# Decayed attention feeding a gated MLP on one core: scores of the first four head pairs in one piece of six banks, and the weight conversions of the start in other places

## The chip, the core and the metric

The kernel runs on 1 core of one Trainium2 chip. The metric is the device time of one execution in microseconds (us), lower is better. Of the kernel before, three runs took 804.63, 805.89 and 807.68 us; the median is 805.89 us. Engines are named as in the profile: PE does matrix products, and transposes as products with an identity matrix, DVE is VectorE, ACT is ScalarE, POOL is GpSimd, and SP issues the transfers (DMA).

## What is computed

The reference has two parts. Attention, for 8 batches of 8 heads with 576 tokens and 64 values each (cut to the core):

```python
scores = scale * np.matmul(q, k.transpose(0, 1, 3, 2))
cum = np.cumsum(np.log(np.clip(f, 0.0001, 1.0)), axis=-1)
scores = np.where(causal, -1e9, scores + cum[..., None] - cum[..., None, :])
attn = np.exp(scores - scores.max(-1, keepdims=True))
attn = attn / (attn.sum(-1, keepdims=True) + 1e-09)
x = np.matmul(attn, v)          # heads side by side: 576 x 512 a batch
```

Then a gated MLP on x of each batch:

```python
h = np.maximum(x @ w_in, 0.0)                  # w_in 512 x 1024
u, v = h[..., :512], h[..., 512:]
v_n = (v - v.mean(-1)) / np.sqrt(v.var(-1) + 1e-06)
v_s = np.einsum('ts,bsd->btd', w_spatial, v_n) + b_spatial[None, :, None]
out = (u * v_s) @ w_out
```

## The kernel before, in words

**Attention.** Two heads of one batch make a pair; there are 32 pairs `P`, four to a batch. `prep(P)` loads the pair's q and k (`qk_t`, 608 KB) and rows of the cumulated decay spread over the partitions (`dk` for each head, `dt` for the last 64 tokens of both), and POOL masks them with `affine_select`. Odd pairs of the first batch have buffers of their own, called `d2`, `t2` and `tl2` (the profile shows them as `d` and `t`); all others share `dk`, `tt` and `tl`.

`scores(P)` takes the queries in blocks of 128, `i` = 0 to 3, with 128(i+1) keys each. PE writes the products into banks `sc`, DVE adds the decay and takes the row minimum in one instruction (`lowest`, line 260), ACT takes the Exp with its row sum (line 298), DVE turns the sums into reciprocals (lines 301 and 302), and `share` (lines 266 and 268) scales the rows. `scores_tail` does the same for the last 64 queries of both heads. `transposes` and `transposes_tail` turn the scaled rows over on PE (`tp`); DVE and ACT copy them by turns into `e` (line 347). `attend` multiplies `e` with v (28 products, line 384), and ACT and DVE split the result into a high part `xh` and a low part `xl` (lines 393 and 394).

In `scores`, the blocks 0, 1 and 2 of both heads make one piece in four banks, and block 3 of both heads makes a second piece, which takes the banks 0 and 1 again once `lowest` has emptied them. `in_one_piece` holds the products of a piece together. `share` is done by ACT for the first two batches and by POOL for the others.

**MLP.** `moe(b)` makes v token tile by token tile (`ps`, five tiles, with the normalisation by DVE, POOL and ACT), then u, then the product with w_spatial (`sph` and `spl`, `spta` and `sptb`), the gate, and the product with w_out. Every operand is a sum of a high and a low part, so a product takes three matmuls.

**Weights.** They come as 64-bit words and are converted on the chip by `load64`: a transfer, an Abs on ACT (line 118), five DVE instructions (lines 119 to 125), an addition on POOL (line 126), a high part by ACT (127) and a low part by POOL (128). `load_first` does four w_in blocks (the half for v) and all of w_spatial during the first batch's attention, and a loop at the end of the kernel deals its steps out between those of `attention(0)`. `load_rest` does the other half of w_in in the v stage of the first batch, and w_out after its u stage.

**What sets the order.** `attention` and `moe` are generators. A loop deals out the steps of batch b's MLP and batch b+1's attention by estimated cost, and a scheduler with a timeline model then orders the instructions of each engine. Each engine and SP work through their own queue in that order, and wait for semaphores at its head. `after(i, mark)` only ties the order, without a wait. The first batch's attention stands in PSUM pools of its own: four banks for `sc` and four for `tp`.

## Time and profile before

One execution was profiled:

| | value |
|---|---|
| time of the profiled execution | 804.53 us |
| its span, first to last instruction | 802.8 us |
| PE busy | 765.6 us, 95% of the span |
| PE weight loads busy | 606.9 us, 76% |
| ACT busy | 438.7 us, 55% |
| DVE busy | 433.3 us, 54% |
| POOL busy | 344.0 us, 43% |
| mean granted PE clock | 0.983 |

The profiled execution was 1.36 us under the median. The span is cut into 40 slices of some 20 us, and for each the page gives the busy tenths of an engine. The chain of waits follows the end of the span back to whatever released each step. An entry such as "L347 ACT COPY e<-tp 128x256 x12 | 4.2, 369" gives line, engine, operation, output and input with shape, count, busy time in us, and the mean of one in ns.

### The profile page before, as it was taken

The numbers are of one execution on the slowest core, as the hardware profiler recorded it, in microseconds if no ns is written. First come the engines' busy times: TensorE is split into PE (matmuls) and PEld (weight loads), VectorE is DVE, ScalarE is ACT, GpSimd is POOL, SyncE is SP. The second block draws the span as 40 slices with busy tenths as digits, with TensorE's granted clock in tenths as the row PEclk, the third lists the DMA queues.
The fourth block names the chain that finished last, engine by engine and source line by source line (L and its number), as shares of the span: only waits on it lengthen the run. The fifth ranks groups of instructions, "written<-read, shape, count | busy, mean of one in ns | idle before, by whom it ended". The sixth has DMA issues, their size and how long they took to land.

```text
span 802.8 us, 14554 instructions
## 1 busy us (share of the span) xinstructions
PE 765.6 (95%) x4934; PEld 606.9 (76%) x4934; DVE 433.3 (54%) x1502; ACT 438.7 (55%) x1172; POOL 344.0 (43%) x641
## 2 busy tenths in 40 slices
PE   7677989899999999999999999999999999999997
PEld 3345668687788777877788878877788867888896
DVE  7846878744744446556564555545554536543322
ACT  3898877765555445545464545544564446542331
POOL 4440573424734335444653337443444436433231
PEclk9789989999999999999999999999999999999999
DMA  8653444223223223233322232332233333201001
GB/s 252 186 176 118 141 135 133 80 92 122 96 96 112 51 96 96 96 123 109 97 93 73 92 109 96 96 107 60 86 89 95 122 118 95 66 24 38 27 1 67
DMA packets 34765, 79.44 MB, mean 99 GB/s; under 512 B 4225, under 2 KB 8321, under 8 KB 34690
## 3 DMA queue, kind: packets, MB, share of 16 engines
q1 hardware_dynamic: 34370, 77.98, 31.5%
q8 instruction: 39, 0.64, 0.3%
q10 hardware_dynamic: 320, 0.52, 0.2%
q14 instruction: 36, 0.29, 0.1%
HBM read 68.73 MB, written 9.75 MB: 98 GB/s over the span
## 4 chain that ended last, share of the span: by engine, by line
PE 73%; DMA 3%; DVE 1%; ACT 1%; issue 1%; POOL 1%; ACTq 0%; POOLq 0%; DVEq 0%; SPq 0%
PE ps L214 42%; PE sc L384 8%; PE sc L285 7%; PE tp L356 7%; PE sc L214 5%; DMA out_dram<-o 3%; PE tp L214 2%; PE tp L368 1%; ACT o L544 1%; DVE tt L260 0%; ACT tt L298 0%; POOL tt L268 0%; DVE w L122 0%; POOL gl L520 0%; DVE wa L121 0%
## 5 line engine op out<-in xcount | busy, mean ns | idle before, releaser
L298 ACT ACTIVATE tt<-tt,nm 128x384 f32<-128x384 f32 (+2 forms) x240 | 133.7, 558 | 85.3 <-DVE nm L260 82.4
L268 POOL TENSOR_SCALAR tt<-tt,sm 128x128 f32<-128x128 f32 x192 | 99.6, 541 | 97.8 <-DVE sm L302 97.1
L520 POOL TENSOR_TENSOR gl<-u,gh 128x256 fp32r<-128x256 f32 (+1 forms) x64 | 51.6, 807 | 145.9 <-ACT gh L519 134.0
L356 PE MATMUL tp<-ident,tt 128*128 128x128 f32 x600 | 105.7, 280 | 7.8 <-DVE e L347 2.7
L384 PE MATMUL sc<-e,vraw 128*64 128x320 f32 (+4 forms) x896 | 97.8, 371 | 7.6 <-ACT e L347 5.9
L356 PEld LDWEIGHTS tp<-ident,tt 128*128 128x128 f32 x600 | 73.5, 141 | 39.8 <-issue 7.4
L384 PEld LDWEIGHTS sc<-e,vraw 128*64 128x64 f32 x896 | 61.4, 141 | 46.9 <-issue 7.0
L347 ACT COPY e<-tp 128x256 f32<-128x256 f32 (+1 forms) x160 | 71.4, 452 | 44.7 <-PE tp L356 41.1
L347 DVE COPY e<-tp 128x384 f32<-128x384 f32 (+1 forms) x160 | 70.7, 445 | 41.7 <-PE tp L356 27.3
L285 PE MATMUL sc<-qk_t 64*128 64x128 f32 (+3 forms) x512 | 89.1, 468 | 3.5 <-DVE nm L260 3.2
L260 DVE CUSTOM_DVE_ANT_1 tt<-sc,dk 128x256 f32<-128x256 f32 (+1 forms) x120 | 66.2, 552 | 47.3 <-PE sc L285 34.2
L214 PE MATMUL ps<-sph,vnh 128*128 128x256 f32 (+1 forms) x240 | 76.3, 318 | 0.8 <-ACT u L494 0.4
L214 PE MATMUL ps<-xh,winh 128*128 128x256 f32 (+1 forms) x232 | 75.7, 326 | 0.0
L214 PE MATMUL ps<-spl,vnh 128*128 128x256 f32 (+1 forms) x240 | 71.5, 298 | 0.0
L214 PE MATMUL ps<-sph,vnl 128*128 128x256 f32 (+1 forms) x240 | 71.2, 297 | 0.0
L214 PE MATMUL ps<-xh,winl 128*128 128x256 f32 (+1 forms) x232 | 70.3, 303 | 0.0
L214 PE MATMUL ps<-xl,winh 128*128 128x256 f32 (+1 forms) x232 | 69.7, 300 | 0.0
L285 PEld LDWEIGHTS sc<-qk_t 64*128 64x128 f32 x512 | 45.1, 190 | 29.9 <-issue 10.5
L214 PE MATMUL ps<-winh,xh 128*128 128x512 f32 x148 | 62.2, 421 | 3.5 <-ACT o L544 2.6
L394 DVE TENSOR_TENSOR xl<-sc,xh 128x256 fp32r<-128x256 f32 x64 | 28.7, 453 | 66.3 <-ACT xh L393 66.3
L214 PE MATMUL ps<-winl,xh 128*128 128x512 f32 x148 | 58.5, 396 | 0.0
L260 DVE CUSTOM_DVE_ANT_0 tt<-sc,dk 128x128 f32<-128x128 f32 (+1 forms) x120 | 49.8, 419 | 13.6 <-PE sc L285 9.7
(179 smaller groups left out, 1721.4 us busy)
## 6 DMA issues: line engine op xcount, KB each, us to landing
qk_t<-in_dram SPq DMA_DIRECT2D x32, 608.0 KB, 5.4
dk<-rows_d SPq DMA_DIRECT2D x60, 320.0 KB, 4.4
vraw<-in_dram SPq DMA_DIRECT2D x32, 320.0 KB, 3.0
dt<-rows_d SPq DMA_DIRECT2D x60, 144.0 KB, 3.5
out_dram<-o SPq DMA_DIRECT2D x32, 256.0 KB, 2.1
w<-in_dram SPq DMA_DIRECT2D x16, 256.0 KB, 3.1
w<-in_dram SPq DMA_DIRECT2D x4, 512.0 KB, 6.4
d<-rows_d SPq DMA_DIRECT2D x4, 320.0 KB, 6.9
```

What stands on the lines that cost most here:

```text
L214: T.matmul(o, l, r, start=st, stop=sp)
L260: return V.tensor_tensor_reduce(out=out, in0=ps, in1=dec, scale=-0.125, scalar=3.0e38, op0=ALU.add, op1=ALU.min, accum_out=acc_)
L268: G.tensor_scalar(out=t, in0=t, scalar1=r, scalar2=1.0, op0=ALU.mult, op1=ALU.mult)
L285: return lambda: T.matmul(ps[:, c:c + n], qk_t[p, n - 128:n], qk_t[p, 640:640 + n], start=True, stop=True)
L298: last["exp", P, h, i] = A.activation(t, t, AF.Exp, bias=nm[h][:, i:i + 1], scale=-1.0, accum_out=sm[h][:, i:i + 1])
L347: copied.setdefault(P, []).append((V.tensor_copy if nev[0] % 2 == 1 else A.copy)(out, ps))
L356: T.transpose(out=tp[:, (i - c) * 128:(i - c + 1) * 128], in_=tt[h][:, TOFF[i] + 128 * c:TOFF[i] + 128 * c + 128], identity=ident)
L368: T.transpose(out=tp[:, j * 128:(j + 1) * 128], in_=tl[:, c * 128:(c + 1) * 128], identity=ident)
L384: return lambda: T.matmul(x[64 * h:64 * h + 64, q0 - s0:q1 - s0], vt[:, c, h, :], e[:, h, e0 + q0:e0 + q1], start=c == 0, stop=c == end)
L394: freed[s0 // 256] = V.tensor_tensor(out=xl[:, s0:s0 + n], in0=ps[:, 0:n], in1=f32(xh[:, s0:s0 + n]), op=ALU.subtract)
L520: G.tensor_tensor(out=gl[j][:, 0:nt], in0=g, in1=f32(gh[j][:, 0:nt]), op=ALU.subtract)
L544: A.copy(o, ps)
```

## The change

It touches the first batch's attention and the weights that are converted beside it.

1. **One piece.** For pairs 0 to 3 all four query blocks of both heads are one piece in six banks: block 3 has the banks 4 and 5. The pool `tp` of that time shrinks from four banks to two. In the code the blocks are taken head by head. In the order that the scheduler makes of it, pair 0 goes partly head by head; in pairs 1 to 3 both heads' 512-wide Exps come first, then both 384-wide ones.
2. **Shares.** For pairs 0 to 3 `share` is done by POOL in place of ACT. Batch 1 keeps ACT.
3. **w_in.** The four blocks of `load_first` are placed at set points of the attention's progress, two of them ahead of the first pair and two after `dk` of pair 0.
4. **Loads.** q and k of pair 1 come after `dk` of pair 0; both `dk` transfers of a pair come ahead of its `dt`; v comes after `dk`.
5. **w_spatial.** It leaves the first batch's attention and is loaded and converted by `load_space` in the five v stages of `moe(0)`, in half rows of 288.

```diff
-    def load_first(ws):
-        for c in range(NJ):
...
+    def load_first(ws, c):
...
+        load64(win_v[:, c, DM:2 * DM, :], winh[:, c, DM:2 * DM], winl[:, c, DM:2 * DM], raw, w[:], t[:],
+               ("dma", 0) if c < 2 else ("dk", 0))
+    def load_space(c):
+        for k0 in (0, 288):
+            raw = mo.tile([128, 288], F32, name="wraw", tag="U", bufs=9)
+            ks = slice(k0, k0 + 288)
+            if c < NB:
+                after(SY.dma_start(out=raw, in_=w_sp[c * 128:(c + 1) * 128, ks]), ("exp", PPB - 1, 1, 0))
+                A.copy(sph[:, c, ks], raw)
+                G.tensor_tensor(out=spl[:, c, ks], in0=raw, in1=f32(sph[:, c, ks]), op=ALU.subtract)
...
         last['dma', P] = SY.dma_start(out=qk_t, in_=qk[P])
+        if P == 1:
+            after(last['dma', P], ('dk', 0))
...
-        SY.dma_start(out=vraw, in_=v[P])
+        after(SY.dma_start(out=vraw, in_=v[P]), ('dk', P))
...
-        if P < 2 * PPB:
+        if PPB <= P < 2 * PPB:
             A.activation(t, t, AF.Copy, scale=r)
...
-        for piece in ((0, 1, 2), (3,)):
+        early = P < PPB
+        for piece in ((0, 1, 2, 3),) if early else ((0, 1, 2), (3,)):
...
-                    at[i, h] = (at[0, h][0], 128) if i == 1 else (bank(i % 3 + h), 0)
+                    n = (4 if early else 0) + h if i == 3 else i + h
+                    at[i, h] = (at[0, h][0], 128, h) if i == 1 else (bank(n), 0, n)
...
+            blocks = [(i, h) for h in range(2) for i in reversed(piece)]
+            for i, h in blocks if early else sorted(blocks, reverse=True, key=lambda x: (x[0], -x[1])):
...
+            if b == 0:
+                load_space(i)
...
-            tc.tile_pool(name="p0t", bufs=4, space=PSUM) as p0t:
+            tc.tile_pool(name="p0t", bufs=2, space=PSUM) as p0t:
...
-            if on and (not won or da <= dw):
+        for c in range(NJ):
+            while da < 0.1 + 0.22 * c:
                 da, on = step(gen, da, t_attn)
-            else:
-                dw, won = step(wgen, dw, 6500.0)
+            load_first(ws, c)
+        while on:
+            da, on = step(gen, da, t_attn)
```

**Where the order moves: PE around the first `attend`.** The rows of before start with pair 0's last transposes for head 1; `t_359` is pair 1's head 0.

```order
L356 MATMUL tp<-ident,tt_83 128x128 x10
L368 MATMUL tp<-ident,tl 128x128 x5
L384 MATMUL sc<-e,vraw 64x320 x2
L384 MATMUL sc<-e,vraw 64x256 x2
L384 MATMUL sc<-e,vraw 64x320 x2
L384 MATMUL sc<-e,vraw 64x128 x2
L384 MATMUL sc<-e,vraw 64x320 x2
L384 MATMUL sc<-e,vraw 64x192 x2
L384 MATMUL sc<-e,vraw 64x64 x2
L356 MATMUL tp<-ident,t_359 128x128 x10
L285 MATMUL sc<-qk_t 128x384 x2
```

In the changed kernel the same place reads as follows; `t_327` is pair 1's head 0.

```order
L375 MATMUL tp<-ident,tl 128x128 x5
L363 MATMUL tp<-ident,t_327 128x128 x3
L391 MATMUL sc<-e,vraw 64x320 x2
L391 MATMUL sc<-e,vraw 64x256 x2
L391 MATMUL sc<-e,vraw 64x320 x2
L391 MATMUL sc<-e,vraw 64x128 x2
L391 MATMUL sc<-e,vraw 64x320 x2
L391 MATMUL sc<-e,vraw 64x192 x2
L391 MATMUL sc<-e,vraw 64x64 x2
L363 MATMUL tp<-ident,t_327 128x128 x7
L292 MATMUL sc<-qk_t 128x512 x2
L292 MATMUL sc<-qk_t 128x384 x2
```

Three transposes of the next pair have moved ahead of `attend`, and the scores of the pair after next begin with the 512-wide products. The same holds for the second and third `attend`.

**POOL between the shares of pair 0 and of pair 1.** Before, POOL had no shares here; `w_345` and `w_412` are w_in blocks, `d_642` and `d_643` pair 3's decay rows.

```order
L128 TENSOR_TENSOR winl<-w_345,winh 128x512
L233 AFFINE_SELECT dk<-dk 128x2x128
L235 AFFINE_SELECT dk<-dk 128x256
L126 TENSOR_TENSOR w_412<-w_412,wa 128x512
L233 AFFINE_SELECT dk<-dk 128x2x128
L235 AFFINE_SELECT dk<-dk 128x256
L233 AFFINE_SELECT d_642<-d_642 128x2x128
L235 AFFINE_SELECT d_642<-d_642 128x256
L128 TENSOR_TENSOR winl<-w_412,winh 128x512
L233 AFFINE_SELECT d_643<-d_643 128x2x128
```

In the changed kernel, `w_586` and `w_760` are the third and fourth w_in block, `d_607` pair 3's decay rows of head 0, `t_327` pair 1's rows to be scaled.

```order
L240 AFFINE_SELECT dk<-dk 128x256
L244 AFFINE_SELECT dt<-dt 64x64
L126 TENSOR_TENSOR w_586<-w_586,wa 128x512
L244 AFFINE_SELECT dt<-dt 64x64
L128 TENSOR_TENSOR winl<-w_586,winh 128x512
L238 AFFINE_SELECT d_607<-d_607 128x2x128
L240 AFFINE_SELECT d_607<-d_607 128x256
L126 TENSOR_TENSOR w_760<-w_760,wa 128x512
L273 TENSOR_SCALAR t_327<-t_327,sm 128x128
L273 TENSOR_SCALAR t_327<-t_327,sm 128x256
L273 TENSOR_SCALAR t_327<-t_327,sm 128x384
L273 TENSOR_SCALAR t_327<-t_327,sm 128x512
```

The shares of pair 1 now stand on POOL behind two w_in blocks and behind pair 3's decay rows.

**ACT where the first batch's attention ends.** Before, the last `xh` of the batch follows the shares of pair 4 (`tt_83`) and three instructions of w_in blocks.

```order
L266 ACTIVATE tl<-tl,sm 128x576
L127 CAST winh<-w_985 128x2x128
L266 ACTIVATE tt_83<-tt_83,sm 128x128
L266 ACTIVATE tt_83<-tt_83,sm 128x256
L266 ACTIVATE tt_83<-tt_83,sm 128x384
L266 ACTIVATE tt_83<-tt_83,sm 128x512
L127 CAST winh<-w_998 128x2x128
L118 ACTIVATE wa<-w_1099 128x256
L393 CAST xh<-sc 128x256
L393 CAST xh<-sc 128x320
```

In the changed kernel:

```order
L271 ACTIVATE tt_82<-tt_82,sm 128x512
L354 COPY e<-tp 128x2x2x64
L271 ACTIVATE tt_83<-tt_83,sm 128x128
L271 ACTIVATE tt_83<-tt_83,sm 128x256
L271 ACTIVATE tt_83<-tt_83,sm 128x384
L271 ACTIVATE tt_83<-tt_83,sm 128x512
L118 ACTIVATE wa<-w_949 128x256
L145 CAST sph<-wraw 128x288 x5
L118 ACTIVATE wa<-w_962 128x256
L145 CAST sph<-wraw 128x288 x2
L400 CAST xh<-sc 128x256
```

The last copy into pair 3's `e` stands behind the shares of pair 4's head 0, and the batch's last `xh` behind seven casts of w_spatial.

More of the change, by code (lines that the diff above doesn't have):

```diff
@@ new lines, in load_first @@
+    def load_first(ws, c):
+        raw = ws.tile([128, DM, 2], U32, name="w64")
+        w = ws.tile([128, DM], U32, name="w32")
+        t = ws.tile([128, DM], U32, name="wa")
+        load64(win_v[:, c, DM:2 * DM, :], winh[:, c, DM:2 * DM], winl[:, c, DM:2 * DM], raw, w[:], t[:],
[8 more added lines that the diff above has]
+                G.tensor_tensor(out=spl[:, c, ks], in0=raw, in1=f32(sph[:, c, ks]), op=ALU.subtract)
+            else:
+                for p0 in (0, 64):
+                    after(SY.dma_start(out=raw[p0:p0 + 64, :], in_=w_sp[TL:S, ks]), ("exp", PPB - 1, 1, 0))
+                A.copy(spta[:, ks], raw)
+                V.tensor_tensor(out=sptb[0:64, ks], in0=raw[0:64, :], in1=f32(spta[0:64, ks]), op=ALU.subtract)
+                br = mo.tile([1, 288], F32, name="br", tag="U", bufs=9)
+                bs = [mo.tile([1, 288], F32R, name=f"bs{r}", tag="U", bufs=9) for r in range(2)]
+                after(SY.dma_start(out=br, in_=b_sp[:, ks]), ("exp", PPB - 1, 1, 0))
+                A.copy(bs[0][:], br)
+                V.tensor_tensor(out=bs[1][:], in0=br, in1=f32(bs[0][:]), op=ALU.subtract)
+                for r in range(2):
+                    SY.dma_start(out=f32(sptb[64 + r:65 + r, ks]), in_=f32(bs[r][:]))
@@ L228, in prep @@
         for h in range(2):
-            SY.dma_start(out=dk[h][:, 0:640], in_=row_of(P, h, 0, 640, 128))
+            last['dk', P] = SY.dma_start(out=dk[h][:, 0:640], in_=row_of(P, h, 0, 640, 128))
+        for h in range(2):
             SY.dma_start(out=dt[64 * h:64 * h + 64, :], in_=row_of(P, h, 640, S, 64))
@@ L291, in scores @@
             yield 250 + 1.68 * 128 * sum(i + 1 for i in piece)
[L292 to L299 removed]
+            blocks = [(i, h) for h in range(2) for i in reversed(piece)]
+            for i, h in blocks if early else sorted(blocks, reverse=True, key=lambda x: (x[0], -x[1])):
+                ps, c, m = at[i, h]
+                n = 128 * (i + 1)
+                t = tt[h][:, TOFF[i]:TOFF[i] + n]
+                freed[m] = lowest(t, ps[:, c:c + n], decay(dk[h], i), nm[h][:, i:i + 1])
+                last["exp", P, h, i] = A.activation(t, t, AF.Exp, bias=nm[h][:, i:i + 1], scale=-1.0,
+                                                    accum_out=sm[h][:, i:i + 1])
         for h in range(2):
@@ L398, in attn_gmlp_kernel, with attention @@
     xs = {}
-    def attention(b, ws=None):
+    def attention(b):
         for P in range(b * PPB, (b + 1) * PPB):
```

41 lines of the change are left out of this document (2 added, 39 removed).

## The prediction

> **What bounds the kernel now.** I read the page's clock line and the stretches first, to find where PE isn't the limit; then the timeline of PE over the first batch; then the groups of ACT, DVE and POOL for prices. Columns of the stretches: PE, PEld, DVE, ACT and POOL busy, then PE clock, DMA share, GB/s.
>
> ```profile
> PEclk9789989999999999999999999999999999999999
> 0.00:20.00 20.00, 15.07 (x67) 6.82 (x68) 14.60 (x24) 7.66 (x11) 9.61 (x20) 1.00 0.82 252
> 20.00:40.00 20.00, 12.93 (x53) 6.81 (x52) 16.13 (x62) 16.94 (x50) 9.94 (x19) 0.74 0.63 186
> 40.00:60.00 20.00, 15.52 (x100) 9.71 (x101) 9.81 (x39) 19.58 (x51) 8.27 (x13) 0.83 0.57 179
> 60.00:80.00 20.00, 15.95 (x120) 11.28 (x116) 12.52 (x54) 17.17 (x50) 1.24 (x4) 1.00 0.37 118
> ```
>
> The clock is below 9 tenths only in the first eight of forty slices, so all that this change can gain or lose lies there: later PE simply works through its list. From 40 to 60 us ACT is the limit (19.58 of 20 us), and POOL is nearly free from 60 on (1.24).
>
> ```profile
> 41.25 4.61 PE L384 MATMUL sc<-e,vraw 128*64 128x320 f32 x28 [2.71 <-ACT e L347]
> 45.79 1.31 PE L356 MATMUL tp<-ident,t 128*128 128x128 f32 x10
> 47.03 1.57 PE L285 MATMUL sc<-qk_t 64*128 64x384 f32 x12
> 48.53 1.31 PE L356 MATMUL tp<-ident,t 128*128 128x128 f32 x10
> 49.68 1.14 PE L214 MATMUL sc<-qk_t 128*128 128x288 f32 x4
> 50.74 1.13 PE L285 MATMUL sc<-qk_t 64*128 64x512 f32 x4
> 51.80 0.77 PE L368 MATMUL tp<-ident,tl 128*128 128x128 f32 x5
> 55.80 4.42 PE L384 MATMUL sc<-e,vraw 128*64 128x320 f32 x28 [3.23 <-ACT e L347]
> 69.13 2.93 PE L384 MATMUL sc<-e,vraw 128*64 128x320 f32 x28 [1.63 <-ACT tl L324]
> 81.46 0.50 PE L214 MATMUL ps<-winh,xh 128*128 128x512 f32 x1
> 85.76 2.93 PE L384 MATMUL sc<-e,vraw 128*64 128x320 f32 x28
> ```
>
> The four `attend` start at 41.25, 55.80, 69.13 and 85.76: a pair takes 14.55, 13.33 and 16.63 us, the last with about 4.2 us of the v stage in it (18 products from 81.46). Two of them wait for copies by ACT, and after 2.71 and 3.23 us of idle the same 28 products take 4.61 and 4.42 us, cold, against 2.93.
>
> **The change part by part.** Start. The decay rows of pair 0 pass through DRAM, and its first `lowest` waits for them:
>
> ```profile
> 12.96 0.33 SPq L229 DMA_DIRECT2D dk<-rows_d x1
> 19.12 0.54 DVE L260 CUSTOM_DVE_ANT_0 tt<-sc,dk 128x384 f32<-128x384 f32 x1
> DMA to landing us min/median/max: 4.1/5.0/6.2
> ```
>
> Four transfers leave the queue ahead of them or move behind `dk` (pair 1's q and k, a piece of w_spatial, v, the third w_in block): over 1 MB, at the 252 GB/s of the first stretch up to 4.8 us. The lower end is no gain. `dk` of pair 0 took 6.2 us from issue to first use, the median landing is 5.0; I take 3 us: first `lowest` at 16.
>
> Shares on POOL. ACT loses eight blocks a pair and POOL gains them:
>
> ```profile
> 57.04 3.71 ACT L266 ACTIVATE tt<-tt,sm 128x128 f32<-128x128 f32 x8
> L268 POOL TENSOR_SCALAR tt<-tt,sm 128x128 f32<-128x128 f32 x192 | 99.6, 541 | 97.8 <-DVE sm L302 97.1
> L235 POOL TENSOR_SCALAR_AFFINE_SELECT dk<-dk 128x256 f32<-128x256 f32 x60 | 25.4, 423 | 0.0
> L126 POOL TENSOR_TENSOR w<-w,wa 128x512 f32<-128x512 f32 x4 | 5.5, 1362 | 9.3 <-DVE wa L125 9.3
> L128 POOL TENSOR_TENSOR winl<-w,winh 128x512 fp32r<-128x512 f32 x4 | 5.3, 1315 | 0.1
> ```
>
> By the order, the first `attend` now stands behind three transposes of pair 1, and these behind pair 1's shares. From POOL's first `dk` mask (about 1 us ahead of the first `lowest`, at 15) to those shares, its queue holds 14 masks of 423 ns (5.9 us), six small ones (an estimate of 1.4, from half that size), three additions of 1362 (4.1), three low parts of 1315 (3.9) and pair 0's eight shares with a tail (8 x 541 ns, and an estimate of 0.7 for the tail from the 541 of its smaller kin: 5.0): 20.3 us, so 35.3. Pair 3's decay rows among them can be fetched only when pair 1's `lowest` has let go of the buffer; I add 0.8 us of waiting (bounds 0 and the 5.0 of a landing). Three shares of 541 and the transposes make 1.9 more: the first `attend` at 38 instead of 41.25, **-3.25**.
>
> One rule of the Trainium skill speaks against putting work on POOL here. First its row: the same instruction on the same tile, free, and beside POOL's subtraction of w_spatial.
>
> ```profile
> 10.63 0.69 DVE L125 SCALAR_TENSOR_TENSOR wa<-w,wa 128x512 f32<-128x512 uint32 x1
> 13.36 1.77 DVE L125 SCALAR_TENSOR_TENSOR wa<-w,wa 128x512 f32<-128x512 uint32 x1
> ```
>
> It costs 1.08 us more. The sum takes nothing for it, since `lowest` reads PSUM; bound: eight such instructions of the third and fourth block, 8.6 us of DVE. "SBUF — State Buffer", section "Who interferes with whom", says that DVE and GpSimd share one pair of ports as an exclusive lock, so that a DVE instruction with two SBUF inputs, or in a two-port mode, waits out GpSimd's. The trace agrees in these two rows; by that rule the conversions between the pairs stretch by up to that bound.
>
> The cycle of a pair. Since the transposes stand ahead of `attend`, one chain runs through: `attend`, scores of the pair after next, `lowest`, Exps, shares, transposes, next `attend`.
>
> ```profile
> L260 DVE CUSTOM_DVE_ANT_1 tt<-sc,dk 128x512 f32<-128x512 f32 x4 | 2.7, 680 | 0.0
> L298 ACT ACTIVATE tt<-tt,nm 128x512 f32<-128x512 f32 x4 | 2.9, 714 | 0.9 <-DVE nm L260 0.9
> L298 ACT ACTIVATE tt<-tt,nm 128x384 f32<-128x384 f32 x4 | 2.4, 612 | 1.0 <-DVE nm L260 1.0
> L298 ACT ACTIVATE tt<-tt,nm 128x256 f32<-128x256 f32 x4 | 2.0, 501 | 0.1
> L298 ACT ACTIVATE tt<-tt,nm 128x128 f32<-128x128 f32 x4 | 1.6, 398 | 0.0
> L324 ACT ACTIVATE tl<-tl,nm 128x576 f32<-128x576 f32 x4 | 3.1, 769 | 0.0
> L347 ACT COPY e<-tp 128x512 f32<-128x512 f32 x8 | 4.6, 579 | 1.1 <-PE tp L356 1.1
> L347 ACT COPY e<-tp 128x256 f32<-128x256 f32 x12 | 4.2, 369 | 0.0
> ```
>
> `attend` 2.93; then 1.24 to the scores as now (45.79 to 47.03) and 0.5 for two `tp` banks instead of four; 1.13 and a handover for the two 512-wide products (1.3); `lowest` 0.7; on ACT eight Exps (2 x 0.714 + 2 x 0.612 + 2 x 0.501 + 2 x 0.398 = 4.45), the tail's 0.77, a wide copy of 0.58 and two narrow of 0.37 (6.5 in all); transposes 0.5. That is 13.7 us; the shares (1.5 after the first head's last Exp) fit beside the tail. The first cycle starts cold (+1.6). In the third, the batch's last copy into `e` stands behind eight Exps and a tail (5.2), copies (1.3), the tail's share (0.8) and half of 3.71 (1.9); with 2.93, 1.74, 1.05 and 0.7 ahead of them, 15.6. Sum 15.3 + 13.7 + 15.6 = 44.6, against 85.76 - 41.25 = 44.5 now: **+0.1**. The scores' single piece and the relief of ACT are eaten by the chain's new order.
>
> v stage. The 18 products are no longer ahead of the fourth `attend`: **+4.2**. And PE has waited some 4 us for that copy, so it starts cold: **+1.6** (bounds 0 and 1.7).
>
> Later pairs, in batch 1:
>
> ```profile
> 107.18 0.55 PE L368 MATMUL tp<-ident,tl 128*128 128x128 f32 x3 [0.76 <-DVE e L347]
> 110.31 0.88 PE L356 MATMUL tp<-ident,tt 128*128 128x128 f32 x2 [2.57 <-ACT tt L266]
> 110.00:115.00 5.00, 4.70 (x17) 3.90 (x19) 3.91 (x12) 4.98 (x12) 3.51 (x6) 0.51 0.80 243
> 115.00:120.00 5.00, 5.00 (x40) 3.40 (x39) 1.68 (x6) 3.63 (x10) 3.38 (x8) 0.81 0.32 88
> ```
>
> Here PE stands 0.76 + 2.57 us for pair 5's copies and shares, and then runs cold: 0.49 of 4.70 us and 0.19 of 5.00 us. Together 6.6 us. In the new order four tiles of u stand ahead of those transposes instead of one, which covers the wait: **-6.0** (bounds 0, if u waits for its own w_in blocks instead, and -6.6).
>
> w_spatial. Eight casts and subtractions by ACT and POOL, and four DVE instructions, enter the v stage. The casts ahead of the last `xh` fall into the cold `attend`: **+0.3** (bounds 0, and the late loads of the third rival). What they cost at their old place is in ACT's 19.58 us, which no longer decides.
>
> Sum: -3.25 + 0.1 + 4.2 + 1.6 - 6.0 + 0.3 = -3.05. The profiled execution took 804.53 us (span 802.8), 1.36 under the median of 805.89. So 801.5 against its own time, and with half of the scatter back **802.3** against the median, 0.4% less. About 0.5%, 4.0 us, is what a measurement of this kernel can tell from no change.
>
> **The rivals.**
>
> *The chain is loose and PE sets the pace.* If POOL runs ahead, the transposes ahead of `attend` never wait. PE's work for a pair is 2.93 + 1.31 + 1.57 + 1.31 + 1.14 + 1.13 + 0.77 = 10.2 us; at 11, 11 and 13.5 a cycle, 9 us go: 793. For it: ACT has 4.5 us less a pair. Against: eight Exps and the tail must end before the next transposes.
>
> *POOL's ports and the stall of batch 1.* DVE's conversions stretch beside POOL's shares, pair 1's `lowest` comes up to 4 us later, and the first `attend` again near 41: 806. For it: 1.77 against 0.69. Against: DVE has slack between pairs (9.81 of 20 us). The rule quoted above gives this case.
>
> *Late loads of w_spatial (slower).* By SP's order these pieces are issued only after pair 5's first `dk`, which waits for pair 4's last `lowest`, about 4.5 us ahead of the fourth `attend`. Seven casts stand ahead of `xh` on ACT.
>
> ```profile
> wraw<-in_dram SPq DMA_DIRECT2D x4, 288.0 KB, 7.2
> ```
>
> With nine transfers at 0.5 us of issue, and 7.2 us to land, the seventh comes 2.6 us after the end of that `attend`; the last row with the bias, two round trips of about 3 us, then holds the next Relu on the same queue: 8.7 us, 811. It decides if the seventh piece lands over 4.6 us after the start of the fourth `attend`. Against: these pieces have half the size.
>
> That the change doesn't do what it says: the Exps of pairs 1 to 3 are not taken head by head. That is in the sum already.
>
> **How the numbers follow.** Forecast 802.3, chance 0.46, own range 798 to 806; just under half of it lies over 0.5% faster. Loose chain, 793: 0.20. Ports or stall, 806: 0.16, mostly within 0.5%. Late loads, 811: 0.18. Faster by over 0.5%: 0.22 + 0.20 = 0.42; within: 0.24 + 0.12 = 0.36; slower: 0.04 + 0.18 = 0.22. The range of 8 in 10 reaches from 790, past the loose chain, to 811.
>
> **What would show it.** Right: first `attend` near 38, pairs of 13 to 16 us with PE waiting on POOL's shares or ACT's copies ahead of `attend`, no idle of over 2 us near 105 to 112. Wrong: first `attend` before 34, or cycles below 12 (loose chain); DVE's conversions over 1.5 us each at 22 to 36 (ports); ACT waiting over 2 us for `wraw` (late loads). If the copy of the batch's last `e` doesn't wait behind pair 4's shares, the terms +4.2 and +1.6 are wrong.

## The result and the profile after

The changed kernel takes 815.03 us (median of 4 runs, 814.92 to 815.67) against 805.26 us for the kernel before on the same chip: a ratio of 1.0118, 95% interval 1.0094 to 1.0142. That is slower by 1.2%, outside the predicted range. The profiled execution has a span of 813.2 us against 802.8, so 10.4 us are to be found.

The clock line and the stretches of the kernel after, to be held against those of before (columns as there):

```profile
PEclk9689899999999999999999999999999999999999
0.00:20.00 20.00, 17.00 (x67) 7.32 (x68) 12.73 (x32) 8.71 (x17) 7.05 (x21) 1.00 0.74 226
20.00:40.00 20.00, 11.54 (x45) 6.49 (x45) 14.99 (x52) 11.94 (x37) 18.57 (x30) 0.69 0.68 220
40.00:60.00 20.00, 16.57 (x101) 9.98 (x102) 8.65 (x37) 8.69 (x28) 11.72 (x23) 0.80 0.41 107
60.00:80.00 20.00, 16.25 (x116) 10.48 (x113) 13.23 (x59) 12.13 (x38) 6.63 (x16) 1.00 0.21 68
100.00:120.00 20.00, 15.28 (x71) 11.10 (x69) 18.30 (x46) 12.65 (x33) 13.01 (x19) 0.91 0.17 54
```

ACT is relieved as foreseen (8.69 of 20 us at 40 to 60, where it was 19.58). But POOL is now full at 20 to 40 (18.57), and DVE nearly so at 100 to 120 (18.30). Of the kernel before, the prediction read no stretch between 80 and 110 us. Here is the one of 20 us that matters, and its first half:

```profile
100.00:120.00 20.00, 16.67 (x92) 12.08 (x91) 15.47 (x45) 15.64 (x38) 14.76 (x23) 0.83 0.46 133
100.00:110.00 10.00, 6.97 (x37) 4.78 (x35) 9.88 (x28) 7.03 (x18) 7.86 (x11) 1.00 0.36 101
```

Before the change already DVE worked 9.88 of 10 us just ahead of the stall near 110. The prediction did not read that row, and it bears on much of what follows.

PE in the kernel after, from just ahead of the first `attend` to the first product of the v stage:

```profile
38.30 0.47 PE L363 MATMUL tp<-ident,tt 128*128 128x128 f32 x1 [0.91 <-DVE sm L332]
38.56 1.49 PE L375 MATMUL tp<-ident,tl 128*128 128x128 f32 x5
40.57 0.87 PE L363 MATMUL tp<-ident,t 128*128 128x128 f32 x3 [0.52 <-ACT e L354]
41.38 4.52 PE L391 MATMUL sc<-e,vraw 128*64 128x320 f32 x28
...
56.76 3.67 PE L391 MATMUL sc<-e,vraw 128*64 128x320 f32 x28
...
70.89 2.92 PE L391 MATMUL sc<-e,vraw 128*64 128x320 f32 x28
...
82.55 1.30 PE L375 MATMUL tp<-ident,tl 128*128 128x128 f32 x5 [2.11 <-DVE sm L308]
85.81 4.49 PE L391 MATMUL sc<-e,vraw 128*64 128x320 f32 x28 [1.95 <-ACT e L354]
90.23 0.50 PE L216 MATMUL ps<-winh,xh 128*128 128x512 f32 x1
```

The fourth `attend` starts at 85.81, where it started at 85.76 before; it is cold (4.49 against 2.93), and the first v product comes after it. So up to here nothing is gained, and with 18 products (4.2 us) still to do, the kernel is behind. Cut at the first and the fourth `attend`, the span falls into three pieces: start 41.38 (41.25 before), three cycles 44.43 (44.51), and 727.4 behind the fourth `attend` (717.0). All 10.4 us lie in the last: 4.2 for the products, 1.6 for the cold `attend`, and 4.6 more, where the prediction had 5.7 less.

### The profile page after: what moved, and what is told of

Same layout as the page of the kernel before. It is cut to its first block, busy times and chain, and to the rows that moved or that the text cites. A ratio compares the mean times of both kernels' runs of the same rounds, so it can differ in the third digit from the quotient of the medians.

```text
span 813.2 us, 14613 instructions
## 1 busy us (share of the span) xinstructions
PE 771.2 (95%) x4927; PEld 608.4 (75%) x4928; DVE 434.0 (53%) x1504; ACT 421.0 (52%) x1142; POOL 366.3 (45%) x681
## 4 chain that ended last, share of the span: by engine, by line
PE 69%; issue 5%; ACT 3%; DMA 2%; POOL 2%; DVE 2%; POOLq 0%; ACTq 0%; DVEq 0%
PE ps L216 39%; PE sc L391 8%; PE tp L363 7%; PE sc L292 7%; PE sc L216 5%; PE tp L216 2%; DMA out_dram<-o 1%; ACT tt L305 1%; POOL gl L529 1%; PE tp L375 1%; DVE tt L265 1%; POOL tt L273 1%; DMA dt<-rows_d 1%; ACT gh L528 1%; ACT tt L271 0%
## 5 line engine op out<-in xcount | busy, mean ns | idle before, releaser
L305 ACT ACTIVATE tt<-tt,nm 128x384 f32<-128x384 f32 (+3 forms) x240 | 133.6, 558 | 107.0 <-DVE nm L265 105.4
L273 POOL TENSOR_SCALAR tt<-tt,sm 128x128 f32<-128x128 f32 x208 | 109.0, 541 | 118.0 <-DVE sm L309 109.6
L363 PE MATMUL tp<-ident,tt 128*128 128x128 f32 x600 | 113.9, 285 | 19.0 <-ACT e L354 5.7
L265 DVE CUSTOM_DVE_ANT_1 tt<-sc,dk 128x512 f32<-128x512 f32 (+1 forms) x120 | 66.0, 551 | 60.2 <-PE sc L292 44.5
```

Source lines behind the costliest of these rows:

```text
L265: return V.tensor_tensor_reduce(out=out, in0=ps, in1=dec, scale=-0.125, scalar=3.0e38, op0=ALU.add, op1=ALU.min, accum_out=acc_)
L273: G.tensor_scalar(out=t, in0=t, scalar1=r, scalar2=1.0, op0=ALU.mult, op1=ALU.mult)
L305: last["exp", P, h, i] = A.activation(t, t, AF.Exp, bias=nm[h][:, i:i + 1], scale=-1.0, accum_out=sm[h][:, i:i + 1])
L363: T.transpose(out=tp[:, (i - c) * 128:(i - c + 1) * 128], in_=tt[h][:, TOFF[i] + 128 * c:TOFF[i] + 128 * c + 128], identity=ident)
```

## The experiments

The table has all runs, cut in the same way. "Start" is the start of the first `attend`, "cycles" from there to the fourth, "behind" from the fourth to the end of the profiled span; the ratio is to the kernel before, with its 95% interval. In kernels built on that of before, 4.2 us of v products lie in "cycles"; in those built on that of after, "behind".

Two cautions go with it. The three pieces come from one profiled execution of each kernel, which lies up to 2.3 us off the median of its runs (e4: 810.35 against 812.68), so small differences of pieces are rough. And the scheduler lays the whole order anew for each edit: ahead of the first `attend`, PE does no transpose of pair 1 in the kernel before, three in that after, four in e11 and e14, and nine in e5 and e19. A run shows what an edit does together with the order that comes with it.

| run | median us | ratio | start | cycles | behind |
|---|---|---|---|---|---|
| before | 805.26 | | 41.25 | 44.51 | 717.0 |
| after | 815.03 | 1.0118 (1.0094 to 1.0142) | 41.38 | 44.43 | 727.4 |
| e1 after, w_spatial in pairs 2 and 3 | 813.42 | 1.0109 (1.0087 to 1.0131) | 41.99 | 48.67 | 720.3 |
| e6 after, the same behind pair 2's Exps | 812.33 | 1.0085 (1.0065 to 1.0104) | 41.47 | 47.35 | 721.7 |
| e10 e6, low parts on DVE | 813.32 | 1.0101 (1.0084 to 1.0118) | 41.52 | 51.09 | 718.8 |
| e18 after, w_spatial not converted | 814.39 | 1.0112 (1.0086 to 1.0137) | 44.46 | 44.87 | 723.3 |
| e5 before, w_spatial in the v stage | 814.12 | 1.0118 (1.0100 to 1.0136) | 44.70 | 41.69 | 725.3 |
| e19 before, w_spatial not converted | 806.24 | 1.0019 (1.0002 to 1.0036) | 46.29 | 41.80 | 716.3 |
| e2 after, shares on ACT | 816.85 | 1.0153 (1.0134 to 1.0173) | 42.51 | 42.98 | 728.7 |
| e4 after, pair 4's shares on POOL | 812.68 | 1.0097 (1.0074 to 1.0119) | 41.25 | 42.39 | 724.9 |
| e11 after, pair 0's shares on ACT | 807.58 | 1.0041 (1.0025 to 1.0057) | 42.45 | 39.17 | 722.3 |
| e17 e4 and e11 together | 813.29 | 1.0111 (1.0091 to 1.0131) | 41.35 | 39.39 | 732.4 |
| e14 after, POOL's masks behind the shares | 808.19 | 1.0051 (1.0034 to 1.0069) | 41.24 | 39.88 | 723.7 |
| e3 after, two pieces and four `tp` banks | 810.34 | 1.0063 (1.0044 to 1.0081) | 42.51 | 41.37 | 724.7 |
| e12 e3, e4 and e10 together | 807.46 | 1.0038 (1.0017 to 1.0058) | 42.37 | 42.56 | 720.4 |
| e9 e4, w_spatial behind the 2nd v tile | 812.85 | 1.0091 (1.0070 to 1.0112) | 41.94 | 44.83 | 724.2 |
| e8 e9, all of w_in in the pairs | 812.97 | 1.0106 (1.0081 to 1.0131) | 44.66 | 50.71 | 715.7 |
| e13 before, batch 1's shares on POOL | 808.87 | 1.0041 (1.0024 to 1.0058) | 41.86 | 44.66 | 719.6 |
| e15 after, lighter conversions | 807.12 | 1.0035 (1.0020 to 1.0050) | 41.53 | 44.20 | 717.6 |
| e16 before, lighter conversions | 801.14 | 0.9957 (0.9942 to 0.9973) | 41.23 | 44.75 | 712.1 |

### Where w_spatial is converted

**e1** puts w_spatial back beside the pairs, in whole rows.

```diff
-            if b == 0:
-                load_space(i)
...
-            load_first(ws, c)
+            (load_first, space_first)[k](ws, c)
```

> The changed kernel, with w_spatial converted during the second and third pair (whole rows of 576, as the kernel before did it) and no longer in the v stage. Theory A, w_spatial: its ten loads and twelve casts hold ACT's queue behind transfers at 90 to 103 us, w_in's second half is converted late, and DVE piles up. Then the waits for xh (1.07 us at 94) and for the lowest of pair 5 (2.43 us at 111.6) go, and the kernel takes 807 to 809 us. Theory B, the order: PE comes to the v stage late and cold (85.81 us, 18 products still ahead) whatever is converted there; then 812 to 815. The first four attends stay within 1 us of 41.4, 56.8, 70.9, 85.8 under both.

Behind the fourth `attend` 7.1 us go, and 4.2 come back in the cycles: the time falls little. **e6** moves its loads later, behind the last Exp of the third pair.

```diff
+            after(SY.dma_start(out=raw, in_=w_sp[c * 128:(c + 1) * 128, :]), ("exp", 2, 1, 0))
```

> The changed kernel, with w_spatial converted in whole rows during the third and fourth pair, its loads behind pair 2's last Exp. In the first such run, with it one pair earlier, the second cycle grew from 15.4 to 19.6 us and the fourth attend came at 90.66 in place of 85.81, but what follows it was 7.0 us shorter. Theory A, w_spatial belongs where POOL and ACT have slack (POOL is busy for 6.6 of 20 us from 60 to 80): cycles grow by 1 to 2 us only, the fourth attend comes at 86 to 88, the rest stays 7 us shorter, 807 to 809 us. Theory B, four more subtractions on POOL ahead of its shares cost a pair what they save later, wherever they stand: fourth attend near 90, 812 to 814.

The same picture with smaller numbers: 2.9 more in the cycles, 5.7 less behind. **e10** asks if the subtraction on POOL, between the shares, makes the cycles long.

```diff
-            G.tensor_tensor(out=spl[:, c, :], in0=raw, in1=f32(sph[:, c, :]), op=ALU.subtract)
+            V.tensor_tensor(out=spl[:, c, :], in0=raw, in1=f32(sph[:, c, :]), op=ALU.subtract)
```

> As the run with w_spatial in the third and fourth pair (812.3 us, fourth attend at 88.82), but its four 128x576 subtractions stand on DVE in place of POOL. Theory G, POOL is what made w_spatial dear there (1.46 us each on POOL ahead of masks and shares; 0.75 us on DVE, which has slack): the fourth attend comes at 85.5 to 87, the rest stays, 808.5 to 811 us. Rival, the casts on ACT or the transfers delay the pairs: fourth attend at 88 to 89.5, 811.5 to 814.

It doesn't: on DVE the cycles get 3.7 us longer still. **e5** makes this one move alone, in the kernel before.

```diff
-        for c in range(NB):
-            raw = ws.tile([128, S], F32, name="wraw", bufs=3)
...
+            if b == 0:
+                load_space(i)
```

> The kernel before with only one part of the change: w_spatial converted in the first batch's v stage. Theory A: the same pile-up there, so 809 to 813 us against 805.3, with ACT waiting for wraw between 80 and 105 us. Theory B: what w_spatial leaves free on ACT and POOL in the first pairs is worth as much as it costs later, 804 to 806.

There the move alone costs about as much as the whole change: 8.3 us behind the fourth `attend`, 3.5 at the start, less 2.8 in the cycles. The last two can't be read singly, as nine transposes of pair 1 now stand ahead of the first `attend`; the fourth starts 0.6 us later than before (86.39 against 85.76). Behind it PE waits for `xh`:

```profile
42.33 2.44 PE L359 MATMUL tp<-ident,t 128*128 128x128 f32 x9 [1.08 <-ACT t L269]
...
95.08 0.80 PE L217 MATMUL ps<-winh,xh 128*128 128x512 f32 x1 [2.17 <-ACT xh L396]
```

On ACT `xh` stands there behind three casts, 1.2 us in all. The casts in turn stand behind pair 4's shares, which begin only at 89.41, after ACT has waited 2.44 us for the sums on DVE. So the casts are the smaller part of this wait.

**e9** moves the pieces behind the second v tile (and takes e4's edit, below); **e8** also brings the second half of w_in into the first four pairs.

```diff
-                after(SY.dma_start(out=raw, in_=w_sp[c * 128:(c + 1) * 128, ks]), ("exp", PPB - 1, 1, 0))
+                after(SY.dma_start(out=raw, in_=w_sp[c * 128:(c + 1) * 128, ks]), ("vn", 1))
```

> The changed kernel with pair 4's shares on POOL (as in the run that took 812.7) and w_spatial converted behind the v stage, its loads behind the second tile of v. Theory A, what costs is that twelve casts wait for transfers in ACT's queue ahead of xh and of w_in's second half: the fourth attend at 83.6, then no wait for xh over 0.5 us, 805 to 808 us. Theory D, the work itself is too much for DVE between 95 and 125 us (19.7 of 20 us busy from 100 to 120 in that run), wherever it stands there: 810 to 813.

> As the run before, and w_in's second half is converted during the first four pairs in blocks of 128x512 too, where DVE is busy for 8.7 and 13.2 of 20 us (40 to 60, 60 to 80); w_out follows behind the fourth tile of v. Theory D, DVE's pile from 95 to 125 us is what PE waits for: four blocks of 2.6 us leave it there, the waits of PE between 90 and 165 us fall below 4 us together, and the kernel takes 798 to 803 us if the cycles of the pairs grow by 1 us each. If the conversions stand ahead of lowest and copies in the pairs' chain, cycles grow by 3 us and more, and it takes 805 to 810.

e9 gives nothing over e4 alone. e8 has the second half of w_in out of the v stage (w_spatial is still converted there) and takes 11.7 us less behind the fourth `attend` than after, 8.5 less than e9; it pays 9.6 us for it in start and cycles. By the medians, 812.97 and 812.85, these conversions cost as much in the pairs as in the v stage.

**e18** and **e19** leave the conversion of w_spatial out, in the kernel after and before; the spatial products then multiply zeros.

```diff
+    for d in (sph, spl, spta, sptb):
+        G.memset(f32(d[:]), 0.0)
...
-            if b == 0:
-                load_space(i)
```

> The changed kernel without any conversion of w_spatial: its tiles are filled with zeros by POOL at the very start, so the spatial products multiply zeros; their number and size stay. It gives the whole price of w_spatial in the v stage. Theory E: that price is the 5.6 us by which the stretch behind the fourth attend got longer. Then the four attends stay within 0.5 us of 41.4, 56.8, 70.9 and 85.8, the wait for the last product's xh (1.07) and the ACT waits for wraw are gone, and the median is 809.4. Rival: the stretch is long because the second half of w_in is loaded 9 us later, behind pair 5's rows, whatever ACT does: 814 to 815. Third: both together, and w_in's conversions also come free from POOL's and ACT's queues, 806.

> The kernel before without any conversion of w_spatial, filled with zeros at the start in the same way. It gives the price of w_spatial at its old place, which the prediction took as nothing once the shares had left ACT. Theory: ACT was the limit at 40 to 60 us (19.58 of 20), and five casts of about 0.7 us, three of them there, cost 2 to 3 us between the first and the fourth attend: 802.5 to 803.5. Rival: they lay beside other waits, and the time is that of before within 1 us. Together with the run on the changed kernel: moving w_spatial costs the difference of the two prices, and 5.6 less 2 to 3 would be a net loss of about 3 us.

The fills that I put on POOL at the start spoil both totals. DVE and POOL in e18, then the same DVE instruction in the kernel after:

```profile
3.67 3.39 DVE L79 TENSOR_SCALAR ft<-ft 64x576 f32<-64x576 f32 x1 [2.22 <-DMA ft<-in_dram]
```
```profile
...
3.69 2.02 POOL L104 MEMSET spl<- 128x2304 f32 x1
...
6.17 0.57 POOL L104 MEMSET sptb<- 66x576 f32 x1
```
```profile
3.53 0.45 DVE L79 TENSOR_SCALAR ft<-ft 64x576 f32<-64x576 f32 x1 [2.09 <-DMA ft<-in_dram]
```

The decay, ahead of everything, takes 3.39 us instead of 0.45 beside them, and the first `attend` comes 3.1 us later. In e19 it comes 5.0 later, with nine transposes of pair 1 ahead of it besides the fills. The fourth `attend` in e18, then in e19:

```profile
89.33 4.56 PE L393 MATMUL sc<-e,vraw 128*64 128x320 f32 x28 [1.96 <-ACT e L356]
```
```profile
88.09 2.92 PE L367 MATMUL sc<-e,vraw 128*64 128x320 f32 x28
```

At its new place w_spatial costs 727.4 - 723.3 = 4.1 us behind the fourth `attend`, less than theory E's 5.6. The rival hit the total of e18, but by the fills: 3.1 of its 812.6 us. At its old place it cost 717.0 - 716.3 = 0.7 us behind; what it cost in the cycles is not shown. They are 44.51 - 41.80 = 2.7 us shorter without it, which looks like the theory's 2 to 3, but they begin behind the nine transposes. To the fourth `attend` the fills cost 3.5 us in e18, and in e19 it comes 2.3 us later than before, so by this estimate about 1 us is left for the old place. Without w_spatial in either kernel the rest of the change costs 812.6 - 804.4 = 8.2 us: 1.2 up to the fourth `attend` (89.33 against 88.09) and 7.0 behind it (723.3 against 716.3), of which 5.8 are the products and the cold `attend`. By this pair of runs the move of w_spatial costs the other 2.2 us; e5, in the kernel before and with another order, has 8.9. The runs don't settle which of the two holds.

### The shares, and what holds the first attend

**e2** gives the shares of the first four pairs back to ACT, and **e4** gives those of pair 4 to POOL too.

```diff
-        if PPB <= P < 2 * PPB:
+        if P < 2 * PPB:
```
```diff
-        if PPB <= P < 2 * PPB:
+        if PPB < P < 2 * PPB:
```

> The changed kernel, with the shares of the first four pairs back on ACT. Theory C, POOL's queue delays the start: in the changed kernel pair 0's shares stand behind w_in's low parts and masks on POOL (PE waits 5.42 us for them at 25.0) and pair 1's from 39.49; on ACT they would start some 3 us earlier, and the first attend comes at 38 to 39. But ACT then has 4.5 us more in each cycle: cycles of 16 to 18 us in place of 15.4, 14.1 and 14.9, so 816 to 822 us in all. If POOL's shares do not set the pace of the cycles either, cycles stay below 15.5 and the time is 811 to 813.

> The changed kernel, with the shares of pair 4 (the first of the second batch) on POOL too. The last copy into e of pair 3 then no longer stands behind a tail's and four blocks' shares on ACT (83.0 to 85.4 us): the fourth attend starts at 82.5 to 83.5 in place of 85.81 and runs warm (2.93 in place of 4.49). If that reaches the end: 811 us. Theory A says the v stage's conversions set the pace after it, so that PE waits for them instead: 813.5 to 815, with longer waits for xh near 90.

In e2 the cycles shrink by 1.5, but start and "behind" grow by 1.1 and 1.3, and neither forecast is met. In e4 ACT's copy no longer stands behind pair 4's shares, the fourth `attend` comes 2.2 us earlier and is warm (2.93); the median falls by about 2 us.

**e11** gives only pair 0's shares to ACT (theory C: POOL's queue holds the first `attend`).

```diff
-        if PPB <= P < 2 * PPB:
+        if P == 0 or PPB <= P < 2 * PPB:
```

> The changed kernel, with only pair 0's shares on ACT, which is idle from 21.9 to 25.5 us there. Theory C, POOL's queue sets the first attend (pair 1's shares begin at 39.49 us behind 25.5 us of masks, additions, low parts, pair 0's shares and waits): 5.8 us leave that queue, and the first attend comes at 37.5 to 39.5 in place of 41.4; it then takes 811 to 813 us. Rival, the cold PE, the copies into e and ACT's own queue between 25 and 41 set it: first attend at 41 or later, 814 to 817.

POOL is relieved, and yet the first `attend` is later. POOL:

```profile
37.16 0.41 POOL L238 TENSOR_SCALAR_AFFINE_SELECT d<-d 128x256 f32<-128x256 f32 x1 [4.71 <-DVE sm L332]
```
POOL stands idle for 4.71 us, so its work isn't what holds it here. Pair 1's shares still begin at 39.13, hardly earlier than after's 39.49: in POOL's order they stand behind pair 3's masks, and pair 3's rows are fetched late. So theory C, that POOL's work holds the start, fails. What shrinks is the cycles, to 39.17, and "behind", by 5.1 us; the total of 807.58 lies below both forecasts. The order of the engines changed with the edit, as in e14.

**e14** sets pair 3's masks and the last w_in addition behind pair 1's shares on POOL (theory I).

```diff
-            G.affine_select(out=two, in_=two, compare_op=ALU.is_ge, fill=-8.0 * BIG, base=0,
-                            pattern=[[0, 2], [-1, 128]], channel_multiplier=1)
+            after(G.affine_select(out=two, in_=two, compare_op=ALU.is_ge, fill=-8.0 * BIG, base=0,
+                            pattern=[[0, 2], [-1, 128]], channel_multiplier=1), ('share', P - 2 if P == 3 else -1))
...
```

> The changed kernel, with pair 3's masks on POOL, and the last addition of w_in's first half, put behind pair 1's shares. With pair 0's shares off POOL the first attend did not come earlier (42.45), though POOL then stood idle for 4.7 us: pair 3's rows are fetched only when pair 1's lowest has released the buffer (32.9), their masks start at 37.0 and stand ahead of pair 1's shares. Theory I, that wait sets the start: shares begin at 37.8 (the reciprocals end there) in place of 39.49, the first attend comes at 39.3 to 40.3, 811 to 814 us. Rival, PE's cold transposes and the copies set it: 41 or later, and 814 to 817.

POOL and PE of e14:

```profile
38.23 4.10 POOL L273 TENSOR_SCALAR t<-t,sm 128x128 f32<-128x128 f32 x8 [0.87 <-DVE sm L309]
```
```profile
38.70 0.47 PE L363 MATMUL tp<-ident,tt 128*128 128x128 f32 x1 [0.69 <-DVE sm L332]
38.96 1.50 PE L375 MATMUL tp<-ident,tl 128*128 128x128 f32 x5
40.25 1.06 PE L363 MATMUL tp<-ident,t 128*128 128x128 f32 x4
41.24 4.39 PE L391 MATMUL sc<-e,vraw 128*64 128x320 f32 x28
```

Pair 1's shares start 1.3 us earlier than after's 39.49, and `attend` gains 0.14: pair 0's own transposes and its tail fill PE's queue up to 40.25. The first `attend` has two bounds close to each other, POOL's queue and the transposes of pair 0 with their copies; taking one away shows the other. That the second comes from the two `tp` banks is not shown: e3 has four banks, and its first `attend` starts at 42.51.

What e14 shows beyond its question is larger. It has all the work of the kernel after, on the same engines, and only POOL's order is tied. Yet it takes 808.19 us against 815.03, below both forecasts: the fourth `attend` starts at 81.12, 4.7 us earlier, and 3.7 less follow behind it. ACT in the kernel after, then in e14, the last copy into pair 3's `e` and the first cast of `xh`:

```profile
85.40 0.36 ACT L354 COPY e<-tp 128x256 f32<-128x256 f32 x1
...
93.91 0.36 ACT L400 CAST xh<-sc 128x256 fp32r<-128x256 f32 x1
```
```profile
80.04 0.36 ACT L354 COPY e<-tp 128x256 f32<-128x256 f32 x1
...
86.94 0.37 ACT L400 CAST xh<-sc 128x256 fp32r<-128x256 f32 x1
```

In the kernel after, the copy stands behind the first of pair 4's shares, and `xh` behind seven casts of w_spatial. In e14 the copy comes ahead of those shares, and `xh` behind two casts. So a good part of the loss, some 5.4 us by the ratios, goes with the order that the scheduler laid, by these rows on ACT above all, and not with the work that was moved.

**e17** joins e4 and e11.

```diff
-        if PPB <= P < 2 * PPB:
+        if P == 0 or PPB < P < 2 * PPB:
```

> The changed kernel, with pair 0's shares on ACT (807.6 us alone) and pair 4's on POOL (812.7 alone, against 815.0). If both gains add up: 803.5 to 805.5, the fourth attend at 79 to 80 us. Theory H, what is saved in the pairs is eaten behind them: 806 to 809.

The fourth `attend` starts at 80.74, 5.1 us earlier than after, and all of that goes again behind it. PE:

```profile
106.61 0.69 PE L363 MATMUL tp<-ident,tt 128*128 128x128 f32 x2 [4.09 <-ACT e L354]
...
119.54 4.34 PE L391 MATMUL sc<-e,vraw 128*64 128x320 f32 x28 [2.71 <-DVE e L354]
```

### The pieces and the banks

**e3** takes the scores of the first four pairs in two pieces again, with four `tp` banks; **e12** adds e4's shares and e10's w_spatial.

```diff
-        early = P < PPB
+        early = False
...
-            tc.tile_pool(name="p0t", bufs=2, space=PSUM) as p0t:
+            tc.tile_pool(name="p0t", bufs=4, space=PSUM) as p0t:
```

> The changed kernel, with the scores of the first four pairs in two pieces of four banks again, and four banks for the transposes. Theory E, the two banks cost more than the single piece saves: PE's waits for copies into e between 30 and 41 us (0.90, 0.64, 0.41, 0.52 us) go, the first attend comes at 39 to 40, cycles stay, 811 to 813 us. If the single piece carries the cycles: cycles of 16 us and more, 816 to 820. If neither: within 1 us of 815.0.

> What the runs so far favour, together: scores in two pieces with four transpose banks (cycles 3.1 us shorter in sum), pair 4's shares on POOL (4 us), w_spatial in the third and fourth pair with its subtractions on DVE (5.6 us off what follows the fourth attend, 1 to 3 on the cycles). If they add up: fourth attend at 82.5 to 84.5, warm, and 801 to 805 us, about the kernel before. Theory H, work moved out of one stage only fills another (DVE, ACT and POOL together bound the first 165 us): 806 to 810.

e3 shortens the cycles by 3.1 us and lengthens the start by 1.1, so the fourth `attend` comes 1.9 us earlier than after. Pieces and banks were changed together, so it doesn't say which of them does it. e12 is the fastest of the complete kernels built on that of after, beside e11, and still above before.

### DVE behind the fourth attend

**e13** takes the shares of batch 1 from ACT in the kernel before. If ACT's shares and copies made the stall near 110, it goes.

```diff
-        if P < 2 * PPB:
+        if P < PPB:
```

> The kernel before, with the shares of pairs 4 to 7 on POOL in place of ACT. It measures the stall on which the prediction put 6 us: there PE waits 2.57 us at 110.3 for pair 5's shares on ACT, then runs cold. If that wait was ACT's, it goes and with it the cold stretch: 798 to 801 us against 804.7. Theory D, DVE was late there anyway (9.88 of 10 us busy from 100 to 110): 803 to 806.

It stays, at 1.45 us instead of 2.57 and with DVE as the releaser, and DVE is fuller. The kernel gets slower (808.87), which neither forecast had. Shares on POOL also run beside DVE's conversions, some of which take 1.2 to 1.4 us there, so the run doesn't part ACT from DVE cleanly. The stretch and PE of e13:

```profile
100.00:120.00 20.00, 14.31 (x76) 10.48 (x76) 18.70 (x47) 12.18 (x31) 14.56 (x22) 0.91 0.41 119
```
```profile
111.55 0.55 PE L368 MATMUL tp<-ident,tl 128*128 128x128 f32 x3 [1.45 <-DVE e L347]
```

**e15** and **e16** make DVE lighter: in the kernel after and before, four of the five DVE instructions of the sixteen later blocks (w_in's other half and w_out) are left out, so these weights are not the right ones (theory D).

```diff
+        part = len(src.shape) == 4
-        V.tensor_scalar(out=af, in0=af, scalar1=2.0 ** -15, scalar2=None, op0=ALU.max)
+        part or V.tensor_scalar(out=af, in0=af, scalar1=2.0 ** -15, scalar2=None, op0=ALU.max)
...
```

> The changed kernel, with four of the five DVE steps left out in the conversion of the sixteen 256-wide blocks (w_in's second half and w_out; the weights come out wrong): 1.3 us each, 20 us of DVE between 85 and 165 us. Theory D, DVE's queue is what PE waits for there: the kernel takes 805 to 809 us. Rival, the wait is for ACT's queue, the transfers or PE's own order: 812 to 815.

> The kernel before with the same four steps left out (weights wrong). Theory D: the 6 us of stall and cold that the prediction saw at 106 to 119 us go with DVE's load, 797 to 800 us. Rival, ACT's shares and copies hold PE there: 803 to 806.

The stretch of e15, then of e16, and PE's wait that is left in e16:

```profile
100.00:120.00 20.00, 15.25 (x79) 10.82 (x78) 15.89 (x46) 15.85 (x45) 16.33 (x24) 1.00 0.35 109
```
```profile
100.00:120.00 20.00, 17.43 (x98) 12.57 (x98) 13.29 (x36) 17.69 (x45) 16.46 (x25) 0.91 0.52 149
```
```profile
113.54 4.61 PE L384 MATMUL sc<-e,vraw 128*64 128x320 f32 x28 [2.04 <-ACT e L347]
```

The same work less gives 9.8 us behind the fourth `attend` in the kernel after (727.4 to 717.6), and 4.9 in that before (717.0 to 712.1); by the ratios it is about 6.7 and 3.5 us. So DVE's load weighs on the pace there, and about twice as hard after the change. Leaving instructions out also shortens the chain of each conversion by itself, and the runs don't part the two. In e16 the wait of 2.57 us at 110 is gone, but one of 2.04 us for ACT's copy stands behind it.

## Why the prediction was wrong

**Start: -3.25 predicted, +0.13 measured.** The mechanism up to the first `lowest` held, and better than predicted: it started at 14.46 (16 predicted). What failed is the step from POOL's queue to the first `attend`. DVE and POOL of the kernel after:

```profile
14.46 0.69 DVE L265 CUSTOM_DVE_ANT_1 tt<-sc,dk 128x512 f32<-128x512 f32 x1 [1.05 <-POOL dk L238]
```
```profile
24.61 2.04 POOL L273 TENSOR_SCALAR tt<-tt,sm 128x128 f32<-128x128 f32 x4
...
27.13 3.04 POOL L273 TENSOR_SCALAR tt<-tt,sm 128x128 f32<-128x128 f32 x4
...
37.02 0.89 POOL L238 TENSOR_SCALAR_AFFINE_SELECT d<-d 128x256 f32<-128x256 f32 x1
...
39.49 4.07 POOL L273 TENSOR_SCALAR t<-t,sm 128x128 f32<-128x128 f32 x8
```

Pair 1's shares begin at 39.49, where 35.3 plus 0.8 was predicted, so the term was mis-sized by 3.4 us. The queue began 1.0 us earlier than predicted, at 14.01. From there to 39.49 POOL is busy for 21.5 us, where 20.3 were predicted; its own instructions stretch (four shares take 3.04 or 2.04 us, one mask 0.89). And it waits for 4.0 us, where 0.8 were predicted; the largest wait is for pair 0's second row (2.19 us at 16.97). With the 1.9 us that the prediction put between these shares and `attend`, 39.49 gives the measured 41.38. POOL was also taken as the only bound; e11 and e14 show another just below it, pair 0's own transposes and their copies.

**Cycles: +0.1 predicted, -0.08 measured.** The sum is right; whether its inside is, no run shows, and luck may have a part in it. The cycles are 2.7 and 2.8 us shorter without w_spatial in e19 and e5, where the prediction held it to be covered, and 3.1 shorter in e3, where it had 0.5 a cycle for two banks. But the start grows in all three, and to the fourth `attend` there is much less to be seen (1.9 us in e3). e14 and e11 have cycles 4.6 and 5.3 us shorter in another order.

**v products +4.2 and the cold attend +1.6: right.** The first v product follows the fourth `attend` at 90.23, and that takes 4.49 us instead of 2.93, because ACT's last copy stood behind pair 4's shares, as worked out: PE waits 2.11 and 1.95 us there, about the 4 predicted. e4 removes this wait, and its fourth `attend` is warm; the 18 products still come behind it.

**w_spatial: +0.3 predicted, 4.1 at its new place by e18 (5.5 to 5.7 by e1 and e6, on equal work).** The step that failed is that the casts fall into the cold `attend`. The rival of late loads has the mechanism, and its condition came true: the seventh cast, in the pair at 93.25, comes more than 4.6 us after the fourth `attend` began at 85.81. ACT in the kernel after:

```profile
90.30 0.43 ACT L145 CAST sph<-wraw 128x288 fp32r<-128x288 f32 x1 [1.70 <-DMA wraw<-in_dram]
92.04 0.98 ACT L145 CAST sph<-wraw 128x288 fp32r<-128x288 f32 x2 [1.31 <-DMA wraw<-in_dram]
...
100.50 0.43 ACT L150 CAST spta<-wraw 128x288 fp32r<-128x288 f32 x1 [1.46 <-DMA wraw<-in_dram]
```

With two shorter waits for the bias row, of 0.49 and 0.79, ACT stands 5.75 us behind transfers while `xh`, a Relu and copies into `e` queue behind. No single wait is over 2 us, so the test that the prediction named for this rival was set too high. The rival's price of 8.7 us was too high as well. And e14 shows that the price hangs on the order: there `xh` stands behind two casts only.

**Stall of batch 1: -6.0 predicted, between -1.1 (e6) and +1.2 us (e18 against e19) measured.** This is the largest miss, and the step that failed is its reading of the wait: the prediction took the releaser's name, ACT, for the cause and the order of PE as the remedy. But ACT was late there because DVE was. DVE and ACT before:

```profile
107.05 0.67 DVE L260 CUSTOM_DVE_ANT_1 tt<-sc,dk 128x512 f32<-128x512 f32 x1
```
```profile
107.83 0.72 ACT L298 ACTIVATE tt<-tt,nm 128x512 f32<-128x512 f32 x1 [0.62 <-PE tp L368]
```

The last Exp ahead of the shares begins right behind this `lowest`, after 0.62 us in which ACT stands idle, and `lowest` comes at the end of a stretch in which DVE was busy for 9.88 of 10 us. e15 and e16 show what DVE's load is worth there. After the change DVE is fuller (18.30 of 20 us against 15.47), and SP shows a likely reason, before and after:

```profile
72.47 4.05 SPq L114 DMA_DIRECT2D w<-in_dram x3
```
```profile
81.61 0.95 SPq L114 DMA_DIRECT2D w<-in_dram x2
```

The second half of w_in is issued 9.1 us later, behind pair 5's rows, which wait for pair 4's last `lowest`. Its conversions then fall among the v tiles' normalisation and pair 5's `lowest`. PE's waits there, in the kernel after, and DVE ahead of the wait at 111.56:

```profile
94.32 0.50 PE L216 MATMUL ps<-winh,xh 128*128 128x512 f32 x1 [1.07 <-ACT xh L400]
...
111.56 0.75 PE L216 MATMUL sc<-qk_t 128*128 128x288 f32 x2 [2.43 <-DVE nm L265]
...
160.88 0.48 PE L363 MATMUL tp<-ident,tt 128*128 128x128 f32 x1 [3.25 <-DVE e L354]
```
```profile
107.40 1.50 DVE L122 SCALAR_TENSOR_TENSOR w<-w,wa 128x256 uint32<-128x256 uint32 x1
109.67 1.37 DVE L125 SCALAR_TENSOR_TENSOR wa<-w,wa 128x256 f32<-128x256 uint32 x1
...
110.96 0.54 DVE L265 CUSTOM_DVE_ANT_0 tt<-sc,dk 128x384 f32<-128x384 f32 x1
```

The wait of 2.57 us at 110.31 became one of 2.43 at 111.56, for DVE by name: its `lowest` at 110.96 stands behind conversions, and the three steps from 107.40 on take 3.6 us, where the same steps near 89 us take some 1.2. POOL is busy beside them. That is the size of the wait, but no run takes the stretching away. The sign that the prediction named, no idle of over 2 us near 105 to 112, did not come. Another wait of 3.25 us stands at 160.88.

**The other rivals.** The loose chain fell: the shortest cycle is 70.89 - 56.76 = 14.13 us. The ports rival at the start fell too, as DVE's conversions at 22 to 37 take 0.41 to 0.83 us, not 1.5; what it describes may act later, in the rows at 107 to 111. The issue of w_in behind pair 5's rows has not been undone by itself, so how the 4.6 us divide between it, w_spatial's waits and the order on ACT stays open: e18 puts 4.1 on w_spatial at its new place, less the 0.7 that it cost behind at its old one, and leaves 1.2 for the rest. e8 takes that half of w_in out of the stretch and has 8.5 us less there than e9 (1.7 of it because its fourth `attend` is warm), but its start and cycles pay as much.

## What to carry to other kernels

Where a stretch keeps one engine busy for 9.88 of 10 us, price each step that enters it against that engine's queue, whatever engine the waits of PE name; and look at the stretches into which work is moved, not only at those that it leaves. A step taken from a full engine is no gain until the next bound has been priced: in e17 the 5.1 us gained up to the fourth `attend` were given back behind it. Where a scheduler lays the order, the same work can cost 5.4 us more or less by the order alone, as e14 shows; look at what stands ahead of a late instruction in its own queue, and try a tie there, before the move itself is blamed. A transfer moved in the order of a queue moves with everything that is queued ahead of it, so the time of issue after the change is to be worked out for each one, also for those that the change doesn't name.
